# A fused attention, gMLP and MLP kernel: seven products for eight in the MLP's second weight, and part of that weight decoded earlier

## The chip, the cores and the metric

One NeuronCore of a Trainium2 chip runs the whole program in one launch. The metric is the device time in microseconds (us). TensorE (PE) does the matmuls and writes to PSUM; VectorE (DVE), ScalarE (ACT) and GpSimd (POOL) work element by element; SyncE (SP) issues most DMAs, in the order of the program. Each engine works off its own queue in order and waits at semaphores for the others.

## The reference

Three stages on 4 x 448 = 1792 tokens, all in float32. Only the last is touched by the change in its arithmetic:

```python
def _moe2_ref(x, g_ln, w_ch1, w_ch2):
    mu = np.mean(x, axis=-1, keepdims=True)
    var = np.mean((x - mu) ** 2, axis=-1, keepdims=True)
    xn = (x - mu) / np.sqrt(var + 1e-06) * g_ln
    ch = np.maximum(xn @ w_ch1, 0.0) @ w_ch2      # 768 -> 3072 -> 768
    return (x + ch)
```

Ahead of it stand a sigmoid attention (12 heads of 64) and a gated MLP: `u, v = relu(x @ w_in)`, `v` normed and mixed along the tokens by `w_spatial` (the spatial stage), then `(u * v_s) @ w_out` (the projection). The weights come as 64-bit floats.

## The kernel before

**Precision and weights.** Every float32 operand is cut into a high and a low half, and a product is three matmuls (`mm3`, lines 342 to 345: high x high, high x low, low x high). A weight is loaded as raw 64-bit words (768 KB for 128 x 768), decoded to float32 and then split. A decode is `scale` (line 843: two ACT instructions, L389 and L394) and `bits` (line 848: one DVE instruction, L398). `Weights.split` (line 811) makes the high half with an ACT cast (L814) and the low half with a subtraction (L817) on VectorE or GpSimd; where VectorE does it and `defer` is set, the subtraction is queued at the start of the next slot (`end_lows`). `Weights.make` (line 807, L809) forms the sums of weight blocks T1 to T4 that a seven-product scheme needs.

**The MLP.** The 3072 hidden columns are cut into 12 groups of 256. Round one takes 1024 tokens (two halves of 512), round two the other 768 (two of 384). In each round and group, w_ch1 is used by a 2 x 2 scheme of seven products in place of eight (Strassen's in Winograd's form), each of nine matmuls: products A11, A12, S1, S2, S4, S3, A22, whose results become the hidden blocks H11, H12, H21, H22 (`after`, line 1302). The bank XY of a product is shared: S1 follows A12 in one bank, A22 follows S3 in one, so the addition of L1280 must have read it first.

Then w_ch2 is used in steps (`step`, line 1329), each nine matmuls into one of two three-bank accumulators. In round one, groups 0, 1 and 11 (`AHEAD`) take seven steps (`SEVEN`): they need S1 to S4, made on VectorE from the hidden blocks (`s_add`, L1294), a cast (L1265) and a low half (`low`, L1271) for each of seven operands, and after each step a sum of the accumulator into SBUF (`add`, L1361, 1536 columns on VectorE). Groups 2 to 10 (`LATE`) take eight plain steps (`EIGHT`): four operands, four sums. In round two all groups take seven steps with seven sums.

**Order.** `tokens` (line 1427) puts the products of group i and the steps of group i-1 by turns: P0 S0 P1 S1 ... P6 S6 (S7). Each token is a slot; after it, `settle` (line 1558) queues whatever is planned for that slot. `at(g, s)` is slot 14 g + s. For a late group, w_ch1 is decoded about slots -9 and -7 of its own stretch and split in slots -6 to 6; w_ch2 is decoded at slots 11 and 13 and split from slot 12 on, lines 1519 to 1530: the low halves on VectorE, the blocks T1 to T4 made on GpSimd and split only for round two (`staged`). Round two fetches all split weights from the DRAM scratch `wscr`, up to 8 slots ahead, into nine blocks that are used in turn.

**Before the MLP.** Group 0, 1 and part of 11 are decoded and split during attention. w_ch2 of group 11 is done by `after_stream` (line 1048): two loads, two decodes, seven splits and four makes, one job at each yield of the last w_in products and of the spatial stage (`filled`, line 1091), its split blocks going through two output blocks `PLACE_OUT`.

**The turn to round two.** At stretch 11 the 768 tokens' normed rows are read back (`x_load`, line 1387), split (`x_split`, L1396 on ACT and L1397 on GpSimd, 1152 wide) and combined (`x_make`, L1400 on VectorE); A12 takes the place in which w_ch2's decoded halves lay.

## Time and profile before

| | us |
|---|---|
| time, median of 3 runs | 1049.4 (1049.29 to 1050.7) |
| profiled execution | 1051.18, of which span 1049.4 |
| attention and w_in | 0 to about 260 |
| spatial stage | 260 to 302 |
| projection | 302 to 370 |
| MLP, round one | 370 to 745 |
| MLP, round two | 745 to 1049 |

Times in the profile are microseconds from the start of the span. An engine's busy share tells how much of a stretch it worked, and the wait views tell who ended a wait. A line such as L817 is that of a helper, so it stands for all instructions that the helper records; the tile names on the left tell them apart (`t_all`, `r_all` and `f_all` are three large SBUF tiles, `acc`, `ps` and `psa` lie in PSUM, `q_all` holds raw weights).

### The profile page before, as it was taken

To read this page: it belongs to the slowest core of one execution; us is meant where nothing else is said; L and a number is where in the kernel's file an instruction comes from. 1 tells how busy PE (TensorE), PEld (TensorE's weight loads), DVE (VectorE), ACT (ScalarE), POOL (GpSimd) and SP (SyncE) were. 2 spreads that over 40 slices of the span, in tenths; PEclk is the share of its full clock that TensorE was granted. 3 is DMA by queue.
4 is the path that set the end of the run, shared out by engine and by line. 5 is a ranking of instruction groups with operands and counts; after the bars stand their busy time and mean duration, and the time that the engine had idled before them with its cause. 6 is when DMAs were issued, how large, how long until landed. Compare 5 with 4: busy or idle time off the path is not lost.

```text
span 1049.4 us, 14789 instructions
## 1 busy us (share of the span) xinstructions
PE 1013.9 (97%) x5221; PEld 846.1 (81%) x5221; DVE 761.1 (73%) x997; ACT 500.7 (48%) x825; POOL 307.6 (29%) x264
## 2 busy tenths in 40 slices
PE   8999999999999999999999999998899999999996
PEld 5556676677799988778777787786789999999995
DVE  3769897736766868966677566768787788777776
ACT  5766545535636654655656556644313323332231
POOL 4532322110214712356455564535300021000000
PEclk9999999999899999999999999999799999999998
DMA  8866989566522576666787767865788988888883
GB/s 223 272 201 209 312 295 283 213 204 210 168 81 108 179 284 242 218 253 251 270 286 268 255 248 266 292 228 180 261 337 285 303 287 252 248 250 253 248 250 120
DMA packets 95097, 251.59 MB, mean 240 GB/s; under 512 B 12720, under 2 KB 27056, under 8 KB 94896
## 3 DMA queue, kind: packets, MB, share of 16 engines
q1 hardware_dynamic: 89616, 237.23, 67.6%
q0 software_dynamic: 1760, 7.36, 2.2%
q10 hardware_dynamic: 3648, 6.06, 1.7%
q8 instruction: 42, 0.69, 0.3%
q14 instruction: 31, 0.25, 0.1%
HBM read 163.82 MB, written 86.78 MB: 239 GB/s over the span
## 4 chain that ended last, share of the span: by engine, by line
PE 70%; issue 10%; DVE 6%; POOL 6%; DMA 3%; ACT 3%; SPq 0%; ACTq 0%; POOLq 0%; DVEq 0%
PE ps L343 12%; PE ps L345 11%; PE ps L344 11%; PE acc L343 7%; PE acc L345 7%; PE acc L344 7%; PE psa L553 6%; PE ps L513 5%; POOL f_all L809 3%; POOL t_all L817 2%; PE ps L526 1%; DVE f_all L1361 1%; DVE f_all L1280 1%; ACT t_all L814 1%; DVE t_all L817 1%
## 5 line engine op out<-in xcount | busy, mean ns | idle before, releaser
L1361 DVE TENSOR_TENSOR f_all<-acc,f_all 128x1152 f32<-128x1152 f32 (+1 forms) x133 | 201.4, 1514 | 56.6 <-PE acc L345 56.5
L343 PE MATMUL ps<-r_all,t_all 128*128 128x384 f32 (+1 forms) x426 | 157.0, 369 | 12.0 <-DVE f_all L1280 12.0
L345 PE MATMUL ps<-r_all,t_all 128*128 128x384 f32 (+1 forms) x426 | 156.3, 367 | 0.0
L344 PE MATMUL ps<-r_all,t_all 128*128 128x384 f32 (+1 forms) x426 | 156.1, 366 | 0.0
L1281 ACT ACTIVATE f_all<-f_all 128x512 f32<-128x512 f32 (+1 forms) x72 | 41.8, 581 | 181.6 <-DVE f_all L1280 181.6
L1265 ACT CAST r_all<-f_all 128x384 fp32r<-128x384 f32 (+1 forms) x141 | 78.6, 558 | 87.9 <-DVE f_all L1294 85.3
L1271 DVE TENSOR_TENSOR r_all<-f_all,r_all 128x384 fp32r<-128x384 f32 (+1 forms) x140 | 100.7, 720 | 27.3 <-ACT r_all L1265 26.1
L817 POOL TENSOR_TENSOR t_all<-f_all,t_all 128x384 fp32r<-128x384 f32 x57 | 66.6, 1168 | 150.3 <-ACT t_all L814 147.8
L343 PE MATMUL acc<-r_all,t_all 128*128 128x512 f32 x246 | 98.4, 400 | 3.4 <-DMA t_all<-wscr 3.4
L343 PEld LDWEIGHTS ps<-r_all,t_all 128*128 128x128 f32 x426 | 80.5, 189 | 24.3 <-ACT t_all L814 9.1
L343 PE MATMUL ps<-r_all 128*128 128x512 f32 (+2 forms) x255 | 97.7, 383 | 0.7 <-DVE f_all L693 0.7
L344 PE MATMUL acc<-r_all,t_all 128*128 128x512 f32 x246 | 98.3, 400 | 0.0
L345 PE MATMUL acc<-r_all,t_all 128*128 128x512 f32 x246 | 98.0, 398 | 0.0
L344 PE MATMUL ps<-r_all 128*128 128x512 f32 (+2 forms) x255 | 96.2, 377 | 0.0
L345 PE MATMUL ps<-r_all 128*128 128x512 f32 (+2 forms) x255 | 96.1, 377 | 0.0
L345 PEld LDWEIGHTS ps<-r_all,t_all 128*128 128x128 f32 x426 | 80.5, 189 | 9.2
L344 PEld LDWEIGHTS ps<-r_all,t_all 128*128 128x128 f32 x426 | 80.6, 189 | 8.9
L809 POOL TENSOR_TENSOR f_all<-f_all 128x384 f32<-128x384 f32 x72 | 85.4, 1191 | 2.6 <-DVE t_all L817 0.6
L500 ACT ACTIVATE f_all<-ps,bias_s 128x896 f32<-128x896 f32 x70 | 68.2, 1006 | 34.7 <-PE ps L526 18.4
L343 PE MATMUL acc<-t_all,r_all 128*128 128x384 f32 x225 | 77.1, 343 | 4.2 <-issue 4.0
L345 PE MATMUL acc<-t_all,r_all 128*128 128x384 f32 x225 | 76.7, 341 | 0.0
L344 PE MATMUL acc<-t_all,r_all 128*128 128x384 f32 x225 | 76.4, 339 | 0.0
(201 smaller groups left out, 2053.2 us busy)
## 6 DMA issues: line engine op xcount, KB each, us to landing
t_all<-wscr SPq DMA_DIRECT2D x178, 384.0 KB, 3.8
wscr<-t_all SPq DMA_DIRECT2D x112, 384.0 KB, 2.9
q_all<-in_w SPq DMA_DIRECT2D x42, 768.0 KB, 4.9
wscr<-r_all SPq DMA_DIRECT2D x56, 384.0 KB, 3.9
r_all<-wscr SPq DMA_DIRECT2D x32, 384.0 KB, 3.7
m_all<-in_v SPq DMA_DIRECT2D x24, 256.0 KB, 3.9
yscr<-f_all SPq DMA_DIRECT2D x14, 384.0 KB, 2.3
f_all<-in_k SPq DMA_DIRECT2D x45, 112.0 KB, 3.8
```

What stands on the lines that cost most here:

```text
L343: nc.tensor.matmul(ps, lh, rh, start=first, stop=False, skip_group_check=skip)
L344: nc.tensor.matmul(ps, lh, rl, start=False, stop=False, skip_group_check=skip)
L345: nc.tensor.matmul(ps, ll, rh, start=False, stop=last, skip_group_check=skip)
L500: nc.scalar.activation(af, ps[:, :, :S], AF.Sigmoid, bias=bias_s, scale=1.0 / math.sqrt(D))
L513: nc.tensor.matmul(ps[:, j, :S], a[w][rows, kc], a[x][rows], start=(i == 0), stop=(i == 2))
L553: nc.tensor.matmul(a["ps"][rows, :S], a["v"][:, 4 * j + c], af[:, j], start=(p % 2 == 0 and c == 0), stop=(p % 2 == 1 and c == 2),)
L809: eng.tensor_sub(self.f(m, WHERE[m][name]), self.f(m, a), self.f(m, b))
L817: low.tensor_sub(t[:, 1], x, t[:, 0])
L1265: nc.scalar.copy(t[:, 0], self.rt(name))
L1271: (eng or nc.vector).tensor_sub(t[:, 1], self.rt(name), t[:, 0])
L1281: nc.scalar.activation(t, t, AF.Relu)
L1361: nc.vector.tensor_add(t, x, t)
```

## The change

In round one all groups take seven steps. Two orders alternate: an even group begins with H12 and ends with H22, its step of H11 leaving its result in the accumulator; the odd group that follows begins with H11 in that same accumulator and adds on top. So each group makes six sums, in round two too, apart from the last group of each round, which makes seven. `EIGHT`, the flag `seven` and the swap of the accumulators go.

w_ch2 of a late group is split into its seven blocks by a table per parity (`W2_JOBS`; a trailing v is VectorE, otherwise GpSimd), in slots 12 to 22 of the group's own stretch, none of them staged. For groups 2, 4, 6, 8, 10 and 11 it is decoded beforehand: `after_stream` now makes twelve decodes, stores each as float32 (384 KB) in a new DRAM tile `wfscr`, and is paced by PE time, one step for each 1.15 us, through the last w_in products, the spatial stage and the projection. Each half is loaded back (`load_plain`) three slots before its former decode. The splits of group 11 move to slots 16 to 26 (`LAST_W2`), staged. `x_split` makes its low half in three instructions of 384.

```diff
+SEVEN = [
+    [   ("H12", "21", 1, None, (0, 0)), ("S1", "T1", 0, True, (1, 1)), ("S2", "T2", 1, True, (0, 1)),
+        ("S4", "22", 0, False, (0, 1)), ("S3", "T3", 1, False, (1, 1)), ("H11", "11", 0, True, None),
+        ("H22", "T4", 1, False, (1, 0)), ],
+    [   ("H11", "11", 0, None, (0, 0)), ("S1", "T1", 1, True, (1, 1)), ("S2", "T2", 0, False, (0, 1)),
+        ("S4", "22", 1, False, (0, 1)), ("S3", "T3", 0, False, (1, 1)), ("H12", "21", 1, True, None),
+        ("H22", "T4", 0, False, (1, 0)), ],
+]
+ENDING = [(*t[:4], t[4] or (0, 0)) for t in SEVEN[1]]
...
-EIGHT = [
-    ("H11", "11", 0, True, None),
-    ("H12", "21", 0, False, (0, 0)),
-    ("H21", "11", 1, True, None),
-    ("H22", "21", 1, False, (1, 0)),
-    ("H11", "12", 0, True, None),
-    ("H12", "22", 0, False, (0, 1)),
-    ("H21", "12", 1, True, None),
-    ("H22", "22", 1, False, (1, 1)),
-]
...
+W2_JOBS = [
+    [
+        (-2, "21v"), (-2, "11v"), (-1, "=T1"), (0, "T1v"), (0, "22v"), (0, "=T3"), (1, "=T2"), (2, "T2v"),
+        (4, "T3"), (5, "=T4"), (6, "T4"),
+    ],
+    [
+        (-2, "11v"), (-1, "=T1"), (0, "T1v"), (0, "22v"), (0, "=T3"), (1, "=T2"), (2, "T2v"), (4, "T3"),
+        (6, "21"), (7, "=T4"), (8, "T4"),
+    ],
+]
+LAST_W2 = [
+    (2, "11"), (3, "=T1"), (3, "22"), (4, "=T3"), (4, "T1"), (5, "=T2"), (6, "T2"), (8, "T3"),
+    (9, "21"), (10, "=T4"), (12, "T4"),
+]
+PLAIN_W2 = [NGRP - 1, 2, 4, 6, 8, 10]
+AFTER_US = 1.15
...
+        def load_plain(self, f, blk):
+            self.x[1, f] = blk.ap(WC)
+            nc.sync.dma_start(blk.ap(WC), wfscr[self.g, f])
...
     def after_stream():
...
+        parts = [(g, f) for g in PLAIN_W2 for f in range(2)]
...
+        load(0)
+        load(1)
+        for _ in range(4):
             yield
+        for k, (g, f) in enumerate(parts):
+            yield
+            weights[g].scale(1, f)
+            yield
+            blk = dec_r.next()
+            weights[g].bits(1, f, blk)
+            yield
+            nc.sync.dma_start(wfscr[g, f], blk.ap(WC))
+            load(k + 2)
+            yield
...
+    def go_on(us):
+        owed[0] += us
+        while owed[0] >= AFTER_US:
+            owed[0] -= AFTER_US
+            next(after, None)
...
         def steps(self):
-            return LAST if self.i == 2 * NGRP - 1 else SEVEN if self.seven else EIGHT
+            if self.i == 2 * NGRP - 1:
+                return LAST
+            return ENDING if self.i == NGRP - 1 else SEVEN[self.i % 2]
...
-            ps, h, blk = acc[b ^ swap[0]], self.h[hn], self.w.t[1, wn]
+            if first is None:
+                first = self.i % NGRP == 0
+            ps, h, blk = acc[b], self.h[hn], self.w.t[1, wn]
...
-        eng.tensor_sub(lo, xf[x], hi)
+        for k in range(HK):
+            eng.tensor_sub(lo[:, k], xf[x][:, k], hi[:, k])
...
     for g in LATE:
         for t, m, f in ((-9, 0, 1), (-7, 0, 0), (11, 1, 0), (13, 1, 1)):
-            decodes[m == f].append((at(g, t), m, f, weights[g]))
+            if m and g in PLAIN_W2:
+                plan(at(g, t) - 3, lambda f=f, g=g: weights[g].load_plain(f, dec[2 + f]))
+            else:
+                decodes[m == f].append((at(g, t), m, f, weights[g]))
...
+    g, t = NGRP - 1, 14
+    for f in range(2):
+        plan(t - 2 + f, lambda f=f: weights[NGRP - 1].load_plain(f, dec[2 + f]))
+    put_all(g, t, 1, LAST_W2, True)
...
-        t1 = t0 + 14
-        put_in(t1 - 2, 1, "11", V)
-        put_in(t1, 1, "21", V)
-        put_in(t1 + 2, 1, "12", V)
-        put_in(t1 + 4, 1, "22", V)
-        plan(t1 + 5, make(g, 1, "T1", G), make(g, 1, "T3", G))
-        put_in(t1 + 6, 1, "T1", V, True)
-        plan(t1 + 6, make(g, 1, "T2", G))
-        put_in(t1 + 7, 1, "T3", V, True)
-        plan(t1 + 7, make(g, 1, "T4", G))
-        put_in(t1 + 8, 1, "T2", V, True)
-        put_in(t1 + 9, 1, "T4", V, True)
+        put_all(g, t0 + 14, 1, W2_JOBS[g % 2])
```

In `W2_JOBS`, slot 0 is the first slot of the stretch after the group's own, and "=T1" is a make, "T1" a split.

## Rows read from the trace of the kernel before

**Rows 1.** Page, first part: busy us (share of the span) and instructions.
```profile
PE 1013.9 (97%) x5221; PEld 846.1 (81%) x5221; DVE 761.1 (73%) x997; ACT 500.7 (48%) x825; POOL 307.6 (29%) x264
```
**Rows 2.** Wait table of PE: us in total, times, longest us.
```profile
PE ps L343 <- DVE f_all L1280: 12.0, 8, 4.2
...
PE psa L690 <- DVE r_all L670: 3.6, 1, 3.6
PE acc L343 <- DMA t_all<-wscr: 3.4, 1, 3.4
PE acc L345 <- DVE r_all L817: 1.2, 1, 1.2
```
**Rows 3.** Table by stretch: length, busy PE, PEld, DVE, ACT, POOL, clock, DMA share, GB/s.
```profile
413.60:442.90 29.30, 29.30 (x128) 23.76 (x127) 26.08 (x23) 17.01 (x29) 11.21 (x11) 1.00 0.57 198
481.20:513.85 32.65, 31.53 (x137) 25.33 (x136) 22.23 (x23) 19.69 (x34) 17.51 (x16) 1.00 0.75 266
710.00:745.00 35.00, 30.48 (x121) 24.19 (x119) 31.23 (x21) 13.92 (x21) 19.78 (x9) 0.90 0.46 150
264.00:298.00 34.00, 33.16 (x149) 29.58 (x150) 27.45 (x54) 20.97 (x41) 7.37 (x11) 0.93 0.45 159
...
384.30:413.60 29.30, 29.30 (x129) 23.79 (x127) 22.46 (x24) 14.05 (x24) 3.11 (x3) 1.00 0.82 300
```
**Rows 4.** PE's order of time: start, length, instruction, idle before, releaser.
```profile
470.60 0.47 PE L343 MATMUL ps<-r_all,t_all 128*128 128x512 f32 x1 [1.11 <-DVE f_all L1280]
...
666.66 0.47 PE L343 MATMUL ps<-r_all,t_all 128*128 128x512 f32 x1 [1.13 <-DVE f_all L1280]
```
**Rows 5.** VectorE's order of time, 426 to 449 us.
```profile
427.98 1.42 DVE L1294 TENSOR_TENSOR f_all<-f_all 128x512 f32<-128x512 f32 x1
...
430.75 0.95 DVE L398 SCALAR_TENSOR_TENSOR f_all<-q_all 128x768 uint32<-128x768 uint32 x1
...
443.04 1.76 DVE L1361 TENSOR_TENSOR f_all<-acc,f_all 128x1536 f32<-128x1536 f32 x1
444.71 0.68 DVE L1271 TENSOR_TENSOR r_all<-f_all,r_all 128x512 fp32r<-128x512 f32 x1
445.31 1.35 DVE L817 TENSOR_TENSOR r_all<-f_all,r_all 128x384 fp32r<-128x384 f32 x1
...
448.92 0.56 DVE L817 TENSOR_TENSOR t_all<-f_all,t_all 128x384 fp32r<-128x384 f32 x1 [0.58 <-ACT t_all L814]
```
**Rows 6.** POOL's order of time, 425 to 448 us.
```profile
427.84 1.01 POOL L817 TENSOR_TENSOR t_all<-f_all,t_all 128x384 fp32r<-128x384 f32 x1 [4.18 <-ACT t_all L814]
...
444.90 1.35 POOL L817 TENSOR_TENSOR t_all<-f_all,t_all 128x384 fp32r<-128x384 f32 x1 [0.97 <-ACT t_all L814]
```
**Rows 7.** Turn, 710 to 745: POOL's x splits, VectorE at 717, SyncE's wait.
```profile
L1397 POOL TENSOR_TENSOR r_all<-q_all,r_all 128x1152 fp32r<-128x1152 f32 x3 | 8.5, 2829 | 22.1 <-DMA t_all<-wscr 22.1
...
717.33 3.84 DVE L1400 TENSOR_TENSOR q_all<-q_all 128x1152 f32<-128x1152 f32 x1
...
SPq L1392 <- DVE t_all L817: 8.7, 1, 8.7
```
**Rows 8.** Table by stretch, the three stretches at granted clock 0.50.
```profile
262.09:268.92 6.83, 5.02 (x14) 4.49 (x15) 4.70 (x9) 2.98 (x6) 1.07 (x2) 0.50 0.86 284
733.12:739.96 6.84, 6.19 (x15) 4.83 (x16) 5.95 (x4) 3.68 (x5) 5.82 (x2) 0.50 0.01 1
746.78:753.61 6.83, 5.51 (x14) 4.71 (x15) 2.65 (x2) 1.57 (x2) 2.28 (x1) 0.50 0.99 390
```
**Rows 9.** ACT's groups, 240 to 270 (count, busy us, mean ns, idle); a fetch.
```profile
L814 ACT CAST r_all<-q_all 128x384 fp32r<-128x384 f32 x7 | 3.8, 538 | 6.3 <-DMA wscr<-r_all 5.3 <-DVE q_all L398 1.0
L394 ACT ACTIVATE q_all<-q_all,bias_d 128x768 uint32<-128x768 uint16 x2 | 2.0, 992 | 0.0
L389 ACT ACTIVATE q_all<-q_all 128x768 f32<-128x768 f32 x2 | 1.8, 914 | 0.0
...
t_all<-wscr SPq DMA_DIRECT2D x178, 384.0 KB, 3.8
```

More of the change, by code (lines that the diff above doesn't have):

```diff
@@ L851, in bits, with do @@
             self.x[m, k] = out.bitcast(F32)
-        def do(self, m, job, blocks, high):
+        def do(self, m, job, blocks):
             if job == "-":
@@ L868, in do @@
                 return 0.9
-            if job[0] == "d":
-                self.scale(m, int(job[1]))
-                return 0.9
-            if job[0] == "e":
-                self.bits(m, int(job[1]))
-                return 0.9
-            self.split(m, job, blocks.next(), high or eng.tensor_copy, nc.vector if high else eng)
+            self.split(m, job, blocks.next(), eng.tensor_copy, eng)
             return 0.9
@@ L1048, in after_stream, with load @@
     def after_stream():
-        outs = Ring(R, 0, 0)
-        outs.blocks = [Block(R, o, 2 * HALF) for o in PLACE_OUT]
-        for grp, m in AFTER:
-            for f in range(2):
-                weights[grp].load(m, f, raw_r.next())
-            for _ in range(4):
-                yield
-            for job in AFTER_JOBS.split():
-                tick()
-                end_lows()
-                weights[grp].do(m, job, outs, nc.scalar.copy)
-                yield
-            end_lows()
-        while puts:
-            tick()
-            yield
-    after = after_stream()
+        parts = [(g, f) for g in PLAIN_W2 for f in range(2)]
+        def load(k):
+            if k < len(parts):
+                g, f = parts[k]
+                weights[g].load(1, f, raw_r.next())
+        load(0)
+        load(1)
+        for _ in range(4):
+            yield
+        for k, (g, f) in enumerate(parts):
[8 more added lines that the diff above has]
+            yield
+    after, owed = after_stream(), [0.0]
+    def go_on(us):
[3 more added lines that the diff above has]
+            next(after, None)
     def v_load(b):
@@ L1092, in filled @@
         side = iter(side)
-        for i, _ in enumerate(gen):
+        for i, us in enumerate(gen):
             if not jobs.q:
-                next(after, None)
+                go_on(us or 0.0)
             if i % every == every - 1:
@@ L1131, in sigmoid_attention_gmlp_mlp @@
     for b in range(B):
-        if b == 2:
-            for _ in after:
-                pass
         g_alloc((b + 1) * S)
@@ L1205, in sigmoid_attention_gmlp_mlp @@
             turn(order[j - 2][1], banks)
+        go_on(AFTER_US)
+        if j == 9:
+            for _ in after:
+                pass
     banks_a.__exit__(None, None, None)
@@ L1236, in __init__ @@
             self.n = (3 if self.two else 4) * P
-            self.seven = self.two or i in AHEAD
             self.r, self.h, self.hb = {}, {}, {}
@@ L1271, in low @@
             (eng or nc.vector).tensor_sub(t[:, 1], self.rt(name), t[:, 0])
-            if not self.seven or name in ("S3", "S4"):
+            if name in ("S3", "S4"):
                 self.drop(name)
@@ L1284, in s_add @@
         def s_add(self, name, eng=None, low=None):
-            if not self.seven:
-                return
             a, b, op = {
@@ L1428, in sigmoid_attention_gmlp_mlp @@
     for i in range(1, 2 * NGRP):
-        n_steps = len(hidden[i - 1].steps())
         seq = []
@@ L1432, in sigmoid_attention_gmlp_mlp @@
             seq += [("P", i, k), ("S", i - 1, k)]
-        seq += [("S", i - 1, k) for k in range(7, n_steps)]
         tokens.append(seq)
@@ L1455, in sigmoid_attention_gmlp_mlp @@
                 t += 2
-            elif token[0] != "T" and not (token[0] == "S" and token[2] == 7):
+            elif token[0] != "T":
                 t += 1
@@ L1503, in sigmoid_attention_gmlp_mlp, with put_in, put_all @@
             plan(t, lambda m=m, f=f, w=w: w.bits(m, f, dec[2 * m + f]))
-            first = t + 2
+            first = max(t + 2, 0)
+    def put_in(g, t, m, name, low, stage=False):
+        plan(t, (staged if stage else direct)(g, m, name, low))
+        takes[t] = takes.get(t, 0) + 1
+    def put_all(g, t, m, jobs, stage=False):
+        for k, job in jobs:
+            if job[0] == "=":
+                plan(t + k, make(g, m, job[1:], G))
+            else:
+                put_in(g, t + k, m, job.strip("v"), V if job[-1] == "v" else G, stage)
+    g, t = NGRP - 1, 14
+    for f in range(2):
+        plan(t - 2 + f, lambda f=f: weights[NGRP - 1].load_plain(f, dec[2 + f]))
+    put_all(g, t, 1, LAST_W2, True)
     for g in LATE:
         t0 = at(g, 0)
-        def put_in(t, m, name, low, stage=False):
-            plan(t, (staged if stage else direct)(g, m, name, low))
-            takes[t] = takes.get(t, 0) + 1
         for j, (name, made) in enumerate(
@@ L1623, in sigmoid_attention_gmlp_mlp @@
                 else:
-                    cur.low("S1" if cur.seven else "H21")
-            if k == 7:
-                continue
+                    cur.low("S1")
         settle(t)
```

46 lines of the change are left out of this document (25 added, 21 removed).

## The prediction

> **What bounds the kernel now.** I read the page first: TensorE (PE) is busy 97% of the span [rows 1], so a gain is either less PE work or less PE waiting. The wait table of PE comes second and names all its larger waits: 12.0 us in 8 waits for VectorE's L1280 (the addition that frees a product's bank), one of 3.6 for a L670 subtraction before the spatial stage, one of 3.4 for a fetched weight, one of 1.2 for a weight's low half, L817 [rows 2]. Third, the stage table. Stretch i below is the products of group i with the w_ch2 steps of group i-1; a slot is one of its nine-matmul pieces. The stretch of seven-step group 1 lies at 413.6 to 442.9: 14 slots, PE busy 29.30 of 29.30 us, DVE 26.1 [rows 3], so a slot is 29.33 / 14 = 2.095 us and a matmul 0.233. The stretch of an eight-step group has 15 slots (31.4 us) and takes 32.7, with DVE at 22.2, ACT at 19.7, POOL at 17.5 [rows 3]. The missing 1.1 us is one wait for L1280 before the last product, seen at 470.60 and, six groups on, at 666.66; (666.66 - 470.60) / 6 = 32.68 us a period [rows 4]. So PE sets the pace, VectorE stops it once per group, and the change pays PE time for VectorE time.
>
> **Term A: eight stretches (3 to 10).** Removed per group: one step of nine matmuls, 2.095 us of PE. The old wait goes too: L1280 of product S3 stood behind splits whose copies ACT made late; these now stand elsewhere, and step 5 has no sum in either order. Ahead of L1280 is then only the sum of step 4, done 1.7 us after a slot that is followed by one of 2.1. What comes instead is read from VectorE's queue, start to start: a sum of 1536 columns 1.67 us (443.04 to 444.71), a 512-wide subtraction 0.60 (444.71 to 445.31), a decode (L398) 0.9, a low half (L817) about 0.5 (0.56 for one alone) [rows 5]; L1280 is as wide as the subtraction and taken as 0.60.
> Before: 4 sums 6.7 + 3 L1280 1.8 + 4 low halves of h 2.4 + 4 decodes 3.5 + 8 weight low halves 4.0 = 18.4 us; the row has 22.2, so 3.8 are waits inside instructions. Where they come from is seen at 427.98: a 0.68 us subtraction takes 1.42, as POOL's instruction of 427.84 ends at 428.85 [rows 5, 6].
> After, even group: 6 sums 10.1 + 1.8 + 4 S-additions 2.4 + 7 low halves of h 4.2 + 2 decodes 1.7 + 5 weight low halves 2.5 = 22.7; odd group (4 decodes, 4 low halves): 24.0. POOL goes from 15 instructions to 17 or 18, about 1.05 each, so the waits grow to some 4.5. VectorE would be busy 27.2 to 28.5 of 29.3 us: just enough room, as in the stretch at 413.6, but every order of its queue now counts. ACT gets 3 more casts and loses two decodes in even groups (3.8); from 19.7 it stays under 22 of 29.3.
> I find two places where PE must wait. First, step 0 needs a weight low half that stands behind the sum of the last step and the low half of S1: 1.67 + 0.60 + 0.5 = 2.8 us after that step, while PE's first use of it (the third matmul after one slot) is at 2.1 + 0.47 = 2.56: 0.3 us. The trace has this very queue once, at 443.04: POOL's instruction of 444.90 came between, and PE waited 1.16 us [rows 2, 5, 6]. Second, the low half of T2 stands behind the sum of step 1 and the S4 subtraction: again 1.67 + 0.60 + 0.5 against 2.56, 0.3 us. At either place it is up to 1.8 if both SBUF instructions meet POOL as at 427.98 and 445.31 (1.42 and 1.35 for 0.68 and 0.56). Ends: 0.6 and 3.7 us a stretch. I take 1.16 + 0.3 = 1.5: the first place has its row, and at the second POOL's queue is mostly waiting for ACT. Period 29.33 + 1.5 = 30.8; A = 8 x (32.68 - 30.8) = -15 us (ends -22 and +3).
>
> **Term B: the last stretch and the turn to round two (704 to 765).** Here DVE is busy 31.2 of 35 us [rows 3], because 1152-wide POOL subtractions of 2.83 us make it wait: a 1152-wide VectorE subtraction, 1.4 by the 512-wide one's 0.60, takes 3.84 at 717.33 [rows 5, 7]. That backlog costs 4.2 us of PE at L1280, and it holds SyncE's queue for 8.7 us before an x load (its target still held by a late weight low half), so that later fetches start late and PE waits 3.4 us for one [rows 2, 7]. Both waits were followed by a granted clock of 0.50, the 1.2 GHz level, for 6.8 us each: 15 matmuls in 6.2 busy us, 0.41 instead of 0.233, so 2.7 us lost [rows 8]. The waits of 1.1 us were not followed by that. After: a step less (-2.1). The x splits are cut in three, so VectorE waits for 1 us, not 2.8; the last group's T3 and T4 low halves move from DVE to POOL and come some four slots earlier, so the x load no longer stands behind them. But there are 6 sums for 4, and POOL has 2 low halves more beside the splits. I take the waits from 4.2 to 1.0 and 3.4 to 0.4, the clock loss from 5.3 to 1.5, and add the 1.5 of the new waits: -2.1 - 3.2 - 3.0 - 3.8 + 1.5 = -10.6 us (ends -14, and +1 if nothing clears).
>
> **Term C: decode in the spatial and projection stages (240 to 320).** Removed there: group 11's seven splits, whose copies made ACT wait 5.3 us for the puts of their two output blocks, in order ahead of the casts of the norm [rows 9]; the norm's last subtraction is what PE waits for at 263.9, 3.6 us, with 2.3 us of half clock behind it (14 matmuls in 5.0 busy us) [rows 2, 8]. Added: twelve decodes instead of two, each 0.91 + 0.99 us on ACT, 0.9 on DVE [rows 5, 9], a 768 KB load and a 384 KB store, one per four steps of 1.15 us of PE time. Their cover: DVE is busy 27.5 and ACT 21.0 of 34 us at 264 to 298 [rows 3]; seven or eight decodes there are 7 us of DVE and 14 of ACT, less the splits. Both end near 34: the cover is nearly gone, and ACT's two-instruction blocks stand ahead of casts that VectorE needs. 1.18 MB in 4.6 us is 256 GB/s on top of 159 [rows 3], more than the 390 of the busiest row [rows 8], less what the splits no longer store. SyncE also waits at each store for the decode; behind it are the statistics of the norm, due later. I take -3.0 and -2.3 for the wait and its clock, +1.5 for new waits: -4 us (ends -7, +4).
>
> **Term D: start of the MLP and round two.** Group 11's w_ch2 is now split in slots 16 to 26: 13 us of POOL, which has 3.1 busy in 29.3, but 9 more transfers of 384 KB on top of 300 GB/s [rows 3]: 121 GB/s more, and the staged blocks shorten the fetch lead from 8 slots to 5 or so (10 us against a landing of 3.8 [rows 9]). +1 us (ends 0, +4). In round two 11 sums go; nothing on PE waits for them: 0.
>
> **Sum.** The profiled execution took 1051.2 us, span 1049.4; it lies 1.8 above the median of 1049.4. -15 - 10.6 - 4 + 1 = -28.6: 1022.6 on the profiled scale, **1021 us** against the median.
>
> **Rivals.** (1) Everything hides: waits of 0.6 a stretch, no half clock left: A -22, B -14, C -7, D 0: 1006. For it: the stretch at 413.6 runs with seven sums and no wait. Against: there its weights were fetched, not split. (2) VectorE and POOL together bound the stage. Added up as if only one could run, 17 or 18 POOL instructions of 1.02 (17.3 to 18.4) and VectorE's two-SBUF-input ones (10.8 to 12.0) are 28.1 to 30.5 of 29.3 us, so odd groups cannot keep up, and even ones inherit their lag: period 30.5 + 1.5 = 32.0, A -5, B -5, C 0, D +2: 1041. The chance is kept down by VectorE instructions with one SBUF input, which fill the time between.
> The Trainium skill, page "SBUF — State Buffer", section "Who interferes with whom", says just this: a VectorE instruction with two SBUF inputs and a GpSimd instruction that reads SBUF exclude each other for a whole instruction. The rows at 427.98 and 717.33 agree; the rule speaks against moving low halves from VectorE to POOL, which shifts the lock, not the work.
> (3) Slower: the chain that makes T2 (VectorE's low half of 22, POOL's make, ACT's copy, VectorE's low half) overruns in every group. It decides once the waits of a stretch pass 32.68 - 29.33 = 3.35 us. Three POOL instructions of the next group stand ahead of the make; with two of them late (2.1 us), the second place costs 0.3 + 2.1 + 0.8 and the first 1.8: 5.0 us, period 34.3, A +13, B, C and D +1 each: 1065, more if half clock follows each wait. For it: VectorE at up to 28.5 of 29.3 with three engines in series. Against: the links come to 1.67 + 0.5 + 0.5 + 1.05 + 0.5 + 0.5 = 4.7 us, and 6.3 lie between the end of step 0 and step 2. (4) The weights are not there: a stored half is loaded two or three slots (4.2 to 6.3 us) before its copy against a landing of 3.8 [rows 9], and SyncE's queue waits for POOL's low halves before it. At 2 us in each of five even groups and D +4: 1034.
>
> **How the numbers follow.** Chances: forecast 0.50, (1) 0.14, (2) 0.17, (4) 0.06, (3) 0.10, no change to speak of 0.03. The range must hold the forecast, (2) and (4), and half of (1): 1004 to 1042. Faster by over 0.2% 0.86, within 0.2% (2 us, about what a measurement of this kernel can tell from none) 0.04, slower 0.10.
>
> **What would show it.** Stretches near 30.8 us with waits for L817 at steps 0 and 2 and none for L1280; granted clock 1.00 before the spatial stage and through the turn; no SyncE wait of 8 us; DVE at 26 to 28 of 29 us. Wrong if a stretch passes 32, if PE waits for DMA at 384 to 414, or if spatial banks (L693) stop PE for over 4 us.

## The result, and the profile after

The changed kernel takes 1059.2 us (median of 4; 1058.4 to 1059.9) against 1049.4 before (median of 4 beside it): ratio 1.0092, 95% interval 1.0075 to 1.011. It is 9.9 us slower; 28 us less were forecast. The profiled execution took 1059.89 us, span 1058.1. One execution each of e7 and e10 below took 1964 us (in the profile of e7 nine matmuls took 4.2 us instead of 2.1); their medians leave it out, and e7 has no times by stage.

The page's first part, after (answers [rows 1]):

```profile
PE 1005.4 (95%) x5140; PEld 823.0 (78%) x5140; DVE 800.6 (76%) x1025; ACT 510.8 (48%) x843; POOL 359.7 (34%) x309
```

81 matmuls fewer, nine in each of nine groups, and PE no longer at 97%: the work went, and waiting took its place. Landmarks of PE's order of time, before and after, tell where; S0(g) is the first w_ch2 step of group g:

| start, us | before | after | difference | forecast of the part |
|---|---|---|---|---|
| S0(0), start of the MLP (Term C) | 386.4 | 385.4 | -1.0 | -4 |
| S0(0) to S0(2) (Term D) | 58.5 | 64.4 | +5.9 | +1 |
| S0(2) to S0(10), eight stretches (Term A) | 261.5 | 271.4 | +9.9 | -15 |
| S0(10) to the turn's first output transposition (Term B) | 67.0 | 61.9 | -5.1 | -10.6 |
| rest of the span | 276.0 | 275.0 | -1.0 | 0 |

A stretch takes 271.4 / 8 = 33.9 us where 30.8 was forecast and 32.7 was the old time: 4.6 us of waits on 29.33 us of matmuls, not 1.5. PE's wait table of after (us in total, times, longest; answers [rows 2]):

```profile
PE acc L359 <- ACT t_all L834: 14.1, 22, 1.4
PE acc L360 <- DVE r_all L1297: 7.8, 5, 1.7
...
PE ps L359 <- DVE f_all L1306: 4.2, 5, 2.2
PE acc L361 <- DVE t_all L837: 4.0, 9, 1.3
PE ps L359 <- DVE f_all L709: 2.2, 2, 1.3
...
PE acc L359 <- DVE r_all L1297: 2.2, 1, 2.2
PE acc L359 <- DMA r_all<-wscr: 1.6, 1, 1.6
```

L1306 is the old L1280, L837 the old L817, L834 the copy ahead of it, L1297 a low half of the hidden units, L709 the old L693. The wait of 12.0 us for L1280 fell to 4.2 and the 3.6 before the spatial stage went. In their place stand 22 waits for ACT's copy of a weight, nine for a weight's low half and five of up to 1.7 us for a hidden low half. The table by stretch (columns as in [rows 3]), an odd and an even stretch and the eight together, and last the same eight before:

```profile
484.40:518.50 34.10, 31.13 (x127) 23.12 (x127) 28.66 (x27) 17.66 (x33) 22.58 (x18) 0.95 0.72 264
518.50:552.90 34.40, 30.92 (x127) 23.16 (x127) 30.12 (x29) 20.89 (x37) 20.38 (x17) 0.95 0.59 220
449.80:721.20 271.40, 246.93 (x1009) 185.46 (x1008) 231.47 (x219) 149.76 (x266) 166.48 (x137) 0.95 0.65 239
444.90:706.40 261.50, 252.53 (x1081) 202.76 (x1080) 175.94 (x185) 153.08 (x265) 135.22 (x117) 1.00 0.74 263
```

VectorE's busy time is the 27.2 to 28.5 us forecast and a little more (231.47 / 8 = 28.9), but of a stretch of 33.9, not 29.3. What it waited for in these 271.4 us has changed. VectorE's wait table, after:

```profile
DVE t_all L837 <- ACT t_all L834: 9.9, 14, 1.1
DVE f_all L1384 <- PE acc L361: 7.8, 13, 1.3
DVE f_all L414 <- POOL f_all L829: 6.4, 7, 0.9
DVE r_all L1297 <- ACT r_all L1291: 5.5, 16, 0.8
DVE f_all L414 <- ACT q_all L410: 4.0, 4, 1.0
DVE f_all L1318 <- ACT f_all L1344: 3.9, 4, 2.1
DVE f_all L1306 <- PE ps L361: 0.7, 2, 0.4
```

and its two rows for PE in the same eight stretches of before (444.9 to 706.4):

```profile
DVE f_all L1280 <- PE ps L345: 19.5, 9, 2.6
DVE f_all L1361 <- PE acc L345: 15.8, 9, 4.6
```

Time in which VectorE waits for PE is time that it has in hand. It was 35.3 us and is 8.5, 1.1 us a stretch. VectorE's waits for ACT and POOL are 29.7 us in these rows, and they were no shorter before (38.1 us); that they now reach PE because so little is in hand is a reading that e6 below puts in doubt. Where in a stretch PE waits, its order of time shows (odd stretch up to 510.59, then even):

```profile
483.01 0.40 PE L361 MATMUL ps<-r_all,t_all 128*128 128x512 f32 x1
484.41 0.50 PE L359 MATMUL acc<-r_all,t_all 128*128 128x512 f32 x1 [1.00 <-ACT t_all L834]
...
489.70 0.50 PE L359 MATMUL acc<-r_all,t_all 128*128 128x512 f32 x1 [0.70 <-ACT t_all L834]
...
494.94 0.50 PE L359 MATMUL acc<-r_all,t_all 128*128 128x512 f32 x1 [0.30 <-ACT t_all L834]
...
518.47 0.50 PE L359 MATMUL acc<-r_all,t_all 128*128 128x512 f32 x1 [1.38 <-ACT t_all L834]
...
539.30 0.50 PE L360 MATMUL acc<-r_all,t_all 128*128 128x512 f32 x1 [1.63 <-DVE r_all L1297]
```

Steps 0, 1 and 2 of every stretch wait for 11 or 21, T1 and T2 of w_ch2, and step 4 of even ones for the low half of S3. By starts, less 0.2325 us a matmul, the waits of groups 2 to 9 are 1.4, 1.5, 0.7, 0.3 and 0.4 us at steps 0, 1, 2, 4 and 5 of odd groups, and 1.65, 0.8, 0.7 and 1.9 at steps 0, 1, 2 and 4 of even ones.

### The profile page after: what moved, and what is told of

It reads as the page before. It is cut to its first block, busy times and chain, and to the rows that moved or that the text cites. A ratio compares the mean times of both kernels' runs of the same rounds, so it can differ in the third digit from the quotient of the medians.

```text
span 1058.1 us, 14729 instructions
## 1 busy us (share of the span) xinstructions
PE 1005.4 (95%) x5140; PEld 823.0 (78%) x5140; DVE 800.6 (76%) x1025; ACT 510.8 (48%) x843; POOL 359.7 (34%) x309
## 5 line engine op out<-in xcount | busy, mean ns | idle before, releaser
L1384 DVE TENSOR_TENSOR f_all<-acc,f_all 128x1536 f32<-128x1536 f32 (+1 forms) x138 | 214.5, 1555 | 48.8 <-PE acc L361 47.4
L359 PE MATMUL ps<-r_all,t_all 128*128 128x384 f32 (+1 forms) x432 | 158.8, 368 | 4.2 <-DVE f_all L1306 4.2
L360 PE MATMUL ps<-r_all,t_all 128*128 128x384 f32 (+1 forms) x432 | 158.3, 366 | 0.5 <-POOL r_all L1420 0.5
L361 PE MATMUL ps<-r_all,t_all 128*128 128x384 f32 (+1 forms) x432 | 158.5, 367 | 0.0
L1291 ACT CAST r_all<-f_all 128x512 fp32r<-128x512 f32 (+1 forms) x168 | 95.2, 567 | 128.4 <-DVE f_all L1318 126.0
L1297 DVE TENSOR_TENSOR r_all<-f_all,r_all 128x512 fp32r<-128x512 f32 (+1 forms) x167 | 131.5, 788 | 27.9 <-ACT r_all L1291 26.6
L837 POOL TENSOR_TENSOR t_all<-f_all,t_all 128x384 fp32r<-128x384 f32 x86 | 104.0, 1221 | 119.8 <-ACT t_all L834 105.8
L359 PE MATMUL acc<-r_all,t_all 128*128 128x512 f32 x228 | 92.7, 406 | 16.2 <-ACT t_all L834 14.1
L360 PE MATMUL acc<-r_all,t_all 128*128 128x512 f32 x228 | 91.6, 402 | 8.1 <-DVE r_all L1297 7.8
L359 PE MATMUL ps<-r_all 128*128 128x512 f32 (+2 forms) x249 | 95.1, 382 | 2.2 <-DVE f_all L709 2.2
L361 PE MATMUL acc<-r_all,t_all 128*128 128x512 f32 x228 | 93.1, 408 | 4.0 <-DVE t_all L837 4.0
L829 POOL TENSOR_TENSOR f_all<-f_all 128x384 f32<-128x384 f32 x76 | 91.4, 1211 | 14.1 <-DMA q_all<-xscr 10.3
L1318 DVE TENSOR_TENSOR f_all<-f_all 128x512 f32<-128x512 f32 (+1 forms) x95 | 73.9, 778 | 26.6 <-ACT f_all L1344 26.2
L360 PE MATMUL ps<-r_all 128*128 128x512 f32 (+2 forms) x249 | 93.5, 376 | 0.0
L361 PE MATMUL ps<-r_all 128*128 128x512 f32 (+2 forms) x249 | 93.5, 376 | 0.0
L359 PE MATMUL acc<-t_all,r_all 128*128 128x384 f32 x225 | 76.5, 340 | 4.3 <-issue 4.3
L361 PE MATMUL acc<-t_all,r_all 128*128 128x384 f32 x225 | 76.2, 339 | 0.0
```

The source lines that it names most:

```text
L359: nc.tensor.matmul(ps, lh, rh, start=first, stop=False, skip_group_check=skip)
L360: nc.tensor.matmul(ps, lh, rl, start=False, stop=False, skip_group_check=skip)
L361: nc.tensor.matmul(ps, ll, rh, start=False, stop=last, skip_group_check=skip)
L829: eng.tensor_sub(self.f(m, WHERE[m][name]), self.f(m, a), self.f(m, b))
L837: low.tensor_sub(t[:, 1], x, t[:, 0])
L1291: nc.scalar.copy(t[:, 0], self.rt(name))
```

## The experiments

"Eight" below is S0(2) to S0(10) in the run's profile (271.4 us after, 261.5 before, and 261.4 in e8, which has the same instructions there as before); ratios are against the kernel before beside the run.

**e1_cut_chain.** The makes of w_ch2 write to a place that no copy reads, so T1 to T4 no longer wait for them (they are not the real weights).

```diff
-            eng.tensor_sub(self.f(m, WHERE[m][name]), self.f(m, a), self.f(m, b))
+            at = (0, 1) if m and self.g in LATE else WHERE[m][name]
+            eng.tensor_sub(self.f(m, at), self.f(m, a), self.f(m, b))
...
```

> The changed kernel, but the four makes of w_ch2 of groups 2 to 10 all write to the place of block 12, which nothing splits, and T3 is split from the place of block 22: VectorE, ACT and POOL keep every instruction and size, and only the dependence of the T splits on the makes (and of the makes on the low halves before them) is gone. The MLP's weights are therefore not the real ones. Chain theory (low half on VectorE, make on POOL, cast on ACT, one after another, is what PE waits for at steps 1 and 2): 1.0 to 2.2 us less in each of nine stretches, 1040 to 1050 us. Load theory (VectorE and POOL exclude each other and are simply too busy): no change, 1057 to 1061.

1055.5 us (ratio 1.003 to 1.0073); eight 268.3. This dependence is worth 3 us of the 36.8 that the eight stretches take beyond their matmuls (271.4 - 8 x 29.33). PE's waits in the eight stretches (L839 and L836 are L837 and L834 here):

```profile
PE acc L361 <- DVE t_all L839: 15.1, 10, 1.7
PE acc L359 <- ACT t_all L836: 6.3, 7, 1.3
```

ACT's copies are early now, and VectorE's low half of the same weight is what is late.

**e2_early_loads.** Stored halves loaded at slots 6 and 9 instead of 8 and 10.

```diff
-                plan(at(g, t) - 3, lambda f=f, g=g: weights[g].load_plain(f, dec[2 + f]))
+                plan(at(g, (6, 9)[f]), lambda f=f, g=g: weights[g].load_plain(f, dec[2 + f]))
```

> The changed kernel, with the stored halves of groups 2, 4, 6, 8 and 10 loaded at slots 6 and 9 of the group's stretch in place of 8 and 10. In the changed kernel the cast of block 21 waits 2.85 us for such a load and PE 1.4 us at step 0 of the even group. If the late load is what costs there: 1.3 to 1.8 us in each of five stretches, 1050 to 1053 us. If VectorE's queue is late there anyway: 1057 to 1060.

1064.0 us (1.0107 to 1.0145); eight 276.4. ACT's waits for stored halves (9.2 us in after) are gone from its table, and the even stretches still wait 1.9 us at step 0 and 1.7 at step 2, now for VectorE's low halves. In these stretches rival 4 falls: the load was late, but it hid a queue that was as late.

**e3_old_group_11.** Group 11's w_ch2 decoded and split in the spatial stage as before, the other five groups' decodes behind it.

```diff
-PLAIN_W2 = [NGRP - 1, 2, 4, 6, 8, 10]
+PLAIN_W2 = [2, 4, 6, 8, 10]
...
-    put_all(g, t, 1, LAST_W2, True)
...
```

> The changed kernel, with group 11's w_ch2 split as in the kernel before (in the last w_in products and the spatial stage), and the decodes of the five other groups behind it. Theory: the 16 extra instructions and nine transfers at slots 12 to 28 hold SyncE's queue at POOL's low halves, so that two fetches come late (PE waits 2.2 and 1.6 us at 408 and 416, with half clock between). Then the start of the MLP loses 5 to 6 us: 1053 to 1055, or 1056 if the spatial stage gives 2 back. Rival (the waits there are VectorE's own queue, as the wait table says for the first): 1058 to 1061.

1069.0 us (1.0157 to 1.0191): the MLP starts 14 us later. PE waits 12.5 us for ACT (L760) in the projection, where four decodes now fall instead of one. But S0(0) to S0(2) is 58.5 us, as before the change: Term D's 5.9 us belong to group 11's splits at slots 16 to 26.

**e4_lows_on_pool.** The low halves of 11, 21 and 22 moved from VectorE to POOL.

```diff
-        (-2, "21v"), (-2, "11v"), (-1, "=T1"), (0, "T1v"), (0, "22v"), (0, "=T3"), (1, "=T2"), (2, "T2v"),
+        (-2, "21"), (-2, "11"), (-1, "=T1"), (0, "T1v"), (0, "22"), (0, "=T3"), (1, "=T2"), (2, "T2v"),
...
```

> The changed kernel, with the low halves of blocks 11, 21 and 22 of groups 2 to 10 on POOL in place of VectorE. Chain theory: the makes of T1 and T2 no longer stand behind VectorE's sum, 1 to 2 us less in each of nine stretches: 1042 to 1051. Load theory: POOL gets 2 to 3 instructions more per group, VectorE waits longer for it: 1060 to 1068.

1073.0 us (1.0196 to 1.024); eight 284.8. The eight stretches:

```profile
449.80:734.60 284.80, 254.13 (x1009) 192.55 (x1008) 219.95 (x199) 148.76 (x265) 182.84 (x158) 0.96 0.61 228
```

VectorE is busy 11.5 us less and POOL 16.4 more, and the stretches are 13.4 us longer, with ACT's copies as PE's largest wait (25.6 us). The load expectation has the sign. That POOL makes a half later and that POOL is too full are both readings of this run; it doesn't tell them apart.

**e5_lows_first.** VectorE's low halves issued ahead of a step's sum.

```diff
+            end_lows()
             cell.step(k)
```

> The low halves of w_ch2 on VectorE are issued ahead of the sum of a step, not behind it; nothing else changes. Theory (order of the queue): PE waits at steps 0 and 2 because a low half of 0.5 us stands behind a sum of 1.67 us. Then each such wait falls by up to 1.67 us, the eight stretches from 271.4 to some 255 us, and the kernel comes to about 1043 us. Rival (load: VectorE and POOL together have more to do than a stretch of 29.3 us holds, because a VectorE instruction with two SBUF inputs and one of POOL exclude each other): the waits only change their name, from the low halves to the sums and the additions that free a bank; stretches 268 to 273 us, 1056 to 1061.

1091.8 us (1.0356 to 1.0423). By starts, the wait at step 0 fell from 1.65 and 1.4 us (even, odd) to nearly nothing and 0.95, that at step 2 from 0.7 to 0.1. But step 1 rose in odd groups from 1.5 to over 3, and 5.1 to 5.7 us stand at step 4 in seven of the eight groups: a low half that waits for its copy now holds back sum, additions and hidden low halves behind it (VectorE waits 30.8 us for ACT's copies, after 9.9). The theory was wrong in sign and the rival in size.

**e6_four_sums.** Two of the six sums, those behind steps 3 and 4, left out in groups 2 to 10.

```diff
-            if out:
+            if out and not (self.i in LATE and k in (3, 4)):
```

> In groups 2 to 10 the sums behind steps 3 and 4 are left out (the output lacks these products); the sums ahead of the two places where PE waits, those of steps 6 and 1, stay. VectorE has 3.3 us less in a stretch, four sums as in the kernel before. Load: the stretches fall by most of 3.3 us each where they stand at 33.9, so to some 245 to 252 us for eight, 1033 to 1040. Order of the queue: the waits at steps 0 and 2 stay, for the sums just ahead of them are still there; only the wait at step 4 goes (1.9 us in even stretches): about 262 us, 1050.

1057.0 us (1.0043 to 1.0083); eight 270.3. VectorE is busy 204.3 us instead of 231.5 and PE gains 1.1 in the eight stretches, 2.2 by the medians. The eight stretches, and VectorE's wait table in them:

```profile
449.80:720.10 270.30, 246.41 (x1009) 185.55 (x1008) 204.32 (x203) 149.64 (x265) 164.45 (x137) 1.00 0.65 239
...
DVE f_all L1306 <- PE ps L361: 12.8, 6, 3.4
DVE r_all L1297 <- ACT r_all L1291: 11.4, 19, 1.3
DVE f_all L414 <- POOL t_all L837: 9.2, 7, 1.9
...
DVE f_all L1384 <- PE acc L361: 7.5, 13, 1.1
```

The freed time became waiting, for PE (20.3 us, after 8.5) and for ACT and POOL. Steps 0 to 2 wait about as in after, and so does step 4 of even groups (1.9 us), which the order expectation had going: both expectations missed. The amount of VectorE's work does not set the period by itself, and neither does the time that it has in hand.

**e7_no_makes.** POOL's four makes of w_ch2 left out in groups 2 to 10.

```diff
             if job[0] == "=":
-                plan(t + k, make(g, m, job[1:], G))
+                if g not in LATE:
+                    plan(t + k, make(g, m, job[1:], G))
```

> In groups 2 to 10 POOL's four subtractions that make T1 to T4 of w_ch2 are left out (the splits take what lies there, so the output is not that of the reference). POOL has some 4.2 us less in a stretch and the chain to T2 loses a link. Load by VectorE and POOL together: about 4 us less to share, stretches of 30 to 31 us, eight at 240 to 250, about 1033. Chain alone: no more than the 3 us that came when the makes wrote elsewhere, 268 us, 1056.

1052.7 us (1.0005 to 1.0036): 6 us of the 26 that the load theory looked for, and more than the 3 of the chain alone.

**e8_split_in_three.** The kernel before, with the x splits cut in three.

```diff
-        eng.tensor_sub(lo, xf[x], hi)
+        for k in range(HK):
+            eng.tensor_sub(lo[:, k], xf[x][:, k], hi[:, k])
```

> The kernel before with one part of the change alone: the x splits of the turn to round two are cut in three, 384 columns each. My reckoning of the turn: VectorE waits 1 us and not 2.8 behind each, the waits for the addition that frees a bank (4.2 us) and for a weight (3.4 us) and their half clock go, some 5 to 9 us: 1042 to 1046. Rival: the turn's gain in the kernel after came from the low halves of T3 and T4 of group 11, which are not moved here; then SyncE's queue still waits some 8 us before an x load, and the time stays within 2 us of 1050.

1048.1 us (0.9966 to 0.9992), some 2 us under before, as the rival expected. S0(10) to the turn is 64.1 us instead of 67.0. PE's waits there:

```profile
732.27 0.80 PE L343 MATMUL ps<-r_all,t_all 128*128 128x512 f32 x1 [2.74 <-DVE f_all L1280]
...
746.01 0.76 PE L343 MATMUL acc<-r_all,t_all 128*128 128x512 f32 x1 [4.24 <-DMA t_all<-wscr]
```

The wait of 4.2 us [rows 2] shrinks, that for the fetch does not, and SyncE still waits 9.4 us for a low half before an x load. Alone, then, the split gives 2.9 us of Term B's 5.1, and the step is 2.1.

**e9_w1_later, e10_copy_first, e11_spread** move instructions only. e9: five w_ch1 splits a slot later. e10: also 11's copy ahead of the second decode in odd groups, and T3 a slot later. e11: also group 11's splits over slots 16 to 34, loads at slots 7 and 10, stores a slot later.

```diff
-            put_in(g, t0 + 2 * j - 6, 0, name, G)
+            at_j = t0 + 2 * j - (5 if j < 5 else 6)
+            put_in(g, at_j, 0, name, G)
...
+        if g % 2:
+            later[t0 + 12].insert(0, later[t0 + 12].pop())
...
-    (2, "11"), (3, "=T1"), (3, "22"), (4, "=T3"), (4, "T1"), (5, "=T2"), (6, "T2"), (8, "T3"),
+    (2, "11"), (3, "=T1"), (5, "22"), (6, "=T3"), (8, "T1"), (9, "=T2"), (11, "T2"), (14, "T3"),
...
```

> Five of the seven w_ch1 splits of a group (11, 21, T1, 22, T2), with the makes that go with them, come one slot later; they have six slots of lead. In POOL's queue the makes of w_ch2's T1, T3 and T2 then stand ahead of them and no longer behind them. No work is added or removed. Theory (lead: w_ch2's chain of four engines is too short of time because POOL's make stands behind instructions of the next group that wait for ACT): the waits at steps 0 to 2 (3.2 us in even, 3.5 in odd stretches) fall by some 1 to 1.5 us a stretch, eight stretches from 271 to about 260, 1048. Rival (nothing but the amount of work in VectorE and POOL counts): 269 to 273, 1057 to 1061.

> As the one before, and two more moves in order: in odd groups ACT's copy of w_ch2's 11 comes ahead of its second decode pair (1.8 us) and not behind it; the split of T3 of w_ch2 comes one slot later, so that POOL's make of w_ch1's T4, for which VectorE's decode waits, stands ahead of it. Lead theory: the wait at step 0 of odd stretches (1.4) and that at step 4 of even ones (1.9) shrink by over half; eight stretches about 252 to 256, 1042. Amount of work: nothing, 1057 to 1061.

> As the one before, and the edges: the splits of group 11's w_ch2 spread over slots 16 to 34 (16 to 26 before), stored halves loaded at slots 7 and 10 (8 and 10), and stores issued three slots behind their split, not two, so that SyncE's queue waits less for POOL. Theory: the two late fetches at the start of the MLP (5.9 us) go, as they did where group 11 was split earlier; the even stretch's wait of ACT for a stored half (2.85 us) shrinks: 1034 to 1038. Rival (the stage is short of DMA as such): the fetches stay late, within 3 us of the kernel before it in this batch.

1058.5 (1.0055 to 1.0096), 1052.5 (1.0011 to 1.0037) and 1048.9 us (0.9972 to 0.9995); eight 273.2, 265.8, 265.8. e9 missed (its rival's 1057 to 1061 held): T1's copy came in time and the wait went to low halves. e10 got a third of what it looked for (step 0 of odd groups 1.4 to 0.9 us, step 4 of even ones 1.9 to 1.2). e11 was right on Term D, S0(0) to S0(2) 59.7 us, but gained nothing in the eight stretches. Together they take 10 us off the changed kernel without taking out one instruction: 5.6 in the eight stretches, 4.7 in Term D. PE's waits of e11 in its eight stretches:

```profile
PE acc L361 <- DVE t_all L837: 11.7, 17, 1.3
PE acc L360 <- DVE r_all L1297: 4.2, 6, 1.0
```

and these stretches in the table by stretch:

```profile
443.70:709.50 265.80, 245.06 (x1009) 186.35 (x1008) 234.66 (x219) 149.40 (x266) 164.31 (x137) 1.00 0.69 244
```

ACT's copies are out of the way; VectorE's low halves, as busy as ever, come last.

**e12_low_before_add, e13_decode_later, e14_and_four_sums**, on top of e11: low halves right behind the sum; then a w_ch1 decode one slot later; then, for e14, e6's two sums left out as well.

```diff
             cell.step(k)
+            end_lows()
...
-        for t, m, f in ((-9, 0, 1), (-7, 0, 0), (11, 1, 0), (13, 1, 1)):
+        for t, m, f in ((-8, 0, 1), (-7, 0, 0), (11, 1, 0), (13, 1, 1)):
...
```

> As e11_spread, and the low halves of w_ch2 on VectorE that are due after a step come right behind its sum, ahead of the 512-wide S-addition or low half of the hidden units that stood between (0.7 to 0.9 us). Order theory: the waits at step 0 (0.6 to 0.9) and step 2 (1.0 to 1.5) shrink by 0.7 to 0.9 each; 1.2 to 1.6 us a stretch, 1036 to 1040. Rival (VectorE is short of time as such): the wait moves to the S4 addition's cast, within 3 us of 1049.

> As the one before, and VectorE's decode of the second half of w_ch1 comes one slot later (slot 6), behind the low half of S3 that stood behind it. Order theory: the wait at step 4 of even stretches (1.2 us) goes, some 5 us for four of them: 1032 to 1035; ends: the load that follows the decode comes no later, so nothing is lost. Rival: the next decode's load lands late and ACT waits for it at slot 10: no gain.

> As the one before, with the sums behind steps 3 and 4 of groups 2 to 10 left out (the output lacks these products). If only order and lead set the waits: within 3 us of the kernel before it in this batch, as the same omission gave 2 us in the changed kernel. If with the order right the amount of VectorE's work sets them: 8 us or more below it.

1048.6 (0.9956 to 0.9989), 1049.3 (0.998 to 0.9999) and 1045.0 us (0.9923 to 0.9961); eight 265.6, 266.1, 262.3. Each took away the wait it aimed at (e12: step 0 from 0.6 and 0.9 to 0.1 and 0.3; e13: step 4 of even groups from 1.1 to nothing) and the sum stayed: the waits came back at product S2 and step 1 in e12, for L1306 before the last product in e13. In both it is the rival's figure that held. Two sums are worth 3.8 us here, 1.1 in after: between both expectations.

**e15_one_slot_lead, e16_lead_alone, e17_no_makes.** e15 (on e13) and e16 (on e11) start w_ch2's chain a slot earlier; e17 is e13 with the makes left out as in e7.

```diff
-        (-2, "11v"), (-1, "=T1"), (0, "T1v"), (0, "22v"), (0, "=T3"), (1, "=T2"), (2, "T2v"), (5, "T3"),
+        (-2, "11v"), (-1, "=T1"), (-1, "T1v"), (-1, "22v"), (0, "=T3"), (0, "=T2"), (1, "T2v"), (5, "T3"),
```

> As e13_decode_later, and the front of w_ch2's chain one slot (2.1 us) earlier: T1 needs only the first half of a group's weights, so it is split at slot -1 and not 0, 22 at -1, T2 made at 0 and split at 1; in even groups 11 at -3. The work is the same. Lead theory: the waits for w_ch2's halves at steps 1 and 2 (about 2.3 us in even, 2.9 in odd stretches) go by most, eight stretches from 266 to 246 to 252 us, 1030 to 1036. Rival (VectorE, POOL and ACT are full at the start of a stretch, slots -2 to 3, and whatever is drawn ahead delays the rest): the waits move to the S-additions and the addition that frees a bank; within 3 us of 1049.

> The same lead on top of e11_spread, without the two moves that only shifted waits. Lead theory: 1030 to 1038. Rival: within 3 us of 1049. If this gains and e15_one_slot_lead does not, or the other way round, the place of the low half against the S-addition decides.

> As e13_decode_later, with POOL's four makes of w_ch2 left out in groups 2 to 10 (the splits take what lies there; the output is not that of the reference). The chain loses its middle link and POOL 4 us a stretch. Taken out of the changed kernel they gave 6 us. If the chain or POOL's load set the remaining waits: 250 us or less for the eight stretches, below 1034. If VectorE and ACT alone are full there: no more than 6 us again, 1043.

1054.6 (1.0022 to 1.0048), 1051.7 (0.9992 to 1.0018) and 1045.7 us (0.993 to 0.9959); eight 272.2, 269.1, 262.7. The lead did what it was to do: in e16 the waits at steps 1 and 2 fell from 1.9 and 2.4 us a stretch (even, odd; e11) to 0.4 and 0.5. But PE then waits before product S2, 1.5 and 3.3 us, for a w_ch1 weight. So e16 fits its rival, and e15 is slower than either expectation. In e17 the makes are worth 3.4 us of the eight stretches, as its expectation had it for VectorE and ACT alone being full (no more than 6). PE's waits of e16 in its eight stretches:

```profile
PE ps L359 <- ACT t_all L834: 9.3, 7, 1.7
PE acc L361 <- DVE t_all L837: 4.1, 7, 0.7
```

**e18_both_chains.** e16 with w_ch1's splits back at their old slots, T1 one earlier.

```diff
-            at_j = t0 + 2 * j - (5 if j < 5 else 6)
+            at_j = t0 + (-6, -4, -3, 0, 2, 4, 6)[j]
```

> As e16_lead_alone, with the w_ch1 splits back at their slots of the changed kernel (only T1 one slot earlier, at -3), so that its T2 has four slots of lead again. Order theory: the new wait before product S2 (1.5 us in even, 3.3 in odd stretches) goes, the waits for w_ch2 stay as small as there; eight stretches from 269 to 250 to 255 us, 1033 to 1038. Rival (start of the stretch is full on ACT, VectorE and POOL together): the waits for w_ch2's T1 and 22 come back or the low halves of 21 and 11 are late; 263 us or more, 1045 to 1052.

1069.9 us (1.0167 to 1.0206), a miss. PE's waits for product S2 went; 5.6 (odd) and 6.1 us (even) appeared at step 0, by starts and with the slower matmuls that followed. ACT's order of time at the start of such a stretch, and VectorE's:

```profile
513.78 0.51 ACT L834 CAST t_all<-f_all 128x384 fp32r<-128x384 f32 x1 [2.26 <-POOL f_all L829]
514.20 0.59 ACT L1344 ACTIVATE f_all<-ps 128x512 f32<-128x512 f32 x1
...
514.82 1.11 DVE L1318 TENSOR_TENSOR f_all<-f_all 128x512 f32<-128x512 f32 x1 [2.92 <-ACT f_all L1344]
```

The copy drawn ahead waits 2.26 us for POOL, H21's activation (L1344) stands behind it, and VectorE's S1 addition waits 2.92 us for that, with 21's low half behind it. One copy in the wrong place on ACT here holds up VectorE and, at step 0, PE.

## Why the prediction was wrong

**Term A, the step that failed: "I find two places where PE must wait", 1.5 us a stretch.** The matmuls went as reckoned (2.095 us a step; PE busy 252.5 to 246.9 us in eight stretches), the old L1280 wait went nearly (0.9 us left in the eight stretches, 7.8 before), and VectorE's sum nearly held: 27.2 to 28.5 forecast, 28.9 measured. What failed is the reading of "just enough room". I priced the queue ahead of each of two low halves as if everything before had come in time. Measured, PE waits at five places of odd groups and four of even ones, 4.6 us a stretch, mostly for a copy or a low half that is itself late: ACT and POOL delay VectorE by some 3.7 us a stretch (29.7 / 8), and ACT's copies wait for POOL 22.0 us in the eight (4.3 before, 2.5 in e11). A stretch over 32 us, the first of the prediction's signs of being wrong, is there. The stretch at 413.6 [rows 3] was no model: its weights were fetched, and VectorE waited there 0.9 us for ACT and not once for POOL.

ACT's and POOL's order of time in the odd stretch show how one delay travels:

```profile
481.65 0.62 ACT L1291 CAST r_all<-f_all 128x512 fp32r<-128x512 f32 x1 [1.56 <-DVE f_all L1318]
482.17 0.91 ACT L405 ACTIVATE q_all<-q_all 128x768 f32<-128x768 f32 x1
482.97 0.98 ACT L410 ACTIVATE q_all<-q_all,bias_d 128x768 uint32<-128x768 uint16 x1
483.86 0.91 ACT L834 CAST t_all<-f_all 128x384 fp32r<-128x384 f32 x2
...
484.85 1.85 POOL L837 TENSOR_TENSOR t_all<-f_all,t_all 128x384 fp32r<-128x384 f32 x1 [2.35 <-ACT t_all L834]
486.65 3.53 POOL L829 TENSOR_TENSOR f_all<-f_all 128x384 f32<-128x384 f32 x3
...
489.14 0.93 ACT L834 CAST t_all<-f_all 128x384 fp32r<-128x384 f32 x2 [1.24 <-POOL f_all L829]
```

A cast waits for VectorE, a decode pair of 1.8 us and two copies stand behind it (PE waits for one at 484.41), POOL waits for the copy and then does three makes in a row, 3.53 us where I let one of 1.05 stand in the chain, and ACT waits for those (PE at 489.70).

**Rival 3** has the sign, the place and the price (5.0 us a stretch, 1065; measured 4.6, 1059), and its deciding point of 3.35 us was passed. Its mechanism is right in small part only: cutting the chain in e1 gave 3 us of 36.8, so that its price came so near is partly luck. My "against" for it, 4.7 us of links in 6.3, left out what stands in each of the three queues. **Rival 2** reckoned a stretch of 32.0 us from a sum of 28.1 to 30.5; 33.9 was measured. e6 doesn't test it, for a sum reads `acc` in PSUM and has one SBUF input, so rival 2 leaves it out; e17 does, and with four makes left out (some 4 us of POOL a stretch) a stretch still takes 32.8 us (33.3 in e13). VectorE and POOL excluding each other is a part of the delay, not the bound by itself. **Rival 4**: the stored half is late in even stretches (ACT waited 2.85 us for it at 517.91), yet earlier loads gain nothing (e2); its other part, 4 us at the start of the MLP behind SyncE's queue, is what Term D shows below.

The Trainium skill, page "SBUF — State Buffer", section "Who interferes with whom", says that a VectorE instruction with two SBUF inputs and a GpSimd instruction that reads SBUF exclude each other for a whole instruction. After's VectorE rows agree: from 484.4 to 552.9 us the two-input L1297 takes 1063 ns in the mean and L1318 1059, about 690 alone, while L1306 with one SBUF input stays at 674. In all it is 5.6 us a stretch, the 28.9 measured less 23.35 (the mean of the prediction's 22.7 and 24.0). That alone does not give the period.

**Term D: +1 forecast, +5.9 measured.** The step that failed is the lead of a fetch, taken as 10 us against a landing of 3.8. PE's and SyncE's order of time:

```profile
408.68 0.47 PE L359 MATMUL acc<-r_all,t_all 128*128 128x512 f32 x1 [2.17 <-DVE r_all L1297]
...
416.26 0.50 PE L359 MATMUL acc<-r_all 128*128 128x512 f32 x1 [1.63 <-DMA r_all<-wscr]
...
403.51 0.38 SPq L848 DMA_DIRECT2D t_all<-wscr  x1
...
408.17 3.16 SPq L929 DMA_DIRECT2D wscr<-t_all  x3
411.42 0.42 SPq L848 DMA_DIRECT2D r_all<-wscr  x1
```

The two fetches were issued 5.2 and 4.8 us before use and landed after 5.0 and 4.8. The second stood behind stores that wait for POOL's low halves (SyncE's waits at such stores, over the span: 204.2 us, 161.9 before, 109.4 in e11). The first wait is put down to VectorE's low half, which ended within 0.2 us of that landing, so which of the two ended it the trace leaves open; both waits are gone in e3. The half clock after the first was not in the sum.

**Term B: -10.6 forecast, -5.1 measured.** The step's 2.1, the SyncE wait of 8.7 and the fetch wait of 3.4 went as reckoned, and of the half clock 3.4 us are left of two times 6.8. But PE still waits 1.11 and 2.21 us for L1306 (749.41 and 764.48), where 1.0 was left in the sum, and the new waits are 3.3 us (0.5, 1.4 and 1.4 by starts), not 1.5; they took up what the fetch gave.

**Term C: -4 forecast, -1.0 measured**, and not to be told better: S0(0) lies between 381.6 and 386.8 us in those of the runs above that leave this stage as it is after (386.4 and 386.6 in two profiles of the old one). The 3.6 us wait and its half clock did go; waits for L709 took 3.5 us, where 0.7 stood.

**What stays open.** Why PE still waits some 4 us a stretch in e11 to e13, and whether order can take them away at all. The order and lead expectations of e9, e12, e13, e15, e16 and e18 missed; of the moves only those of e10 shortened the eight stretches. No variant of the changed kernel brought a stretch under 32.8 us, not even with two sums (262.3 / 8) or four makes (262.7 / 8) left out; neither alone sets the period. No run left out both, and none took work from ACT, so that the three engines together are too full where the waits lie is a rival that stands. The best kernels with the whole computation, e12 (1048.6) and the old kernel with its x splits in three (1048.1), lie 2 to 3 us under before: a product saved in each of nine groups has come to nearly nothing.

## What to carry to other kernels

When an edit pays the bound engine's time with another engine's, look at how long that other engine waits for the bound one, and at what else it waits for: 35.3 us for PE here, 8.5 after. This tells how near the two are, not what a delay will cost, for with 20.3 us of it back (e6) PE gained 1.1. A chain over three in-order queues is priced with what stands ahead of it in each, not by its links. To tell amount from order, leave out work and see if time goes, on each engine of the chain: in the same eight stretches 27 us of VectorE gave 1.1 us, and moves alone gave 5.6.
